# State products by head in quarters of the array, gap products grouped by shape, and weights rounded in three VectorE steps and a GpSimd addition

## The chip, the cores and the metric

The kernel runs on one core of one Trainium2 chip. The metric is the device time of one execution in microseconds; before the change it is 642.75 us (median of three runs, 642.05 to 643.14). Lower is better.

## What is computed

A gated linear attention with a recurrent state, and behind it a feed-forward block with the activation h - tanh(h).

```python
# q, k, v, alpha: (4, 8, 768, 48) fp32; alpha in 0.8..1.0
for t in range(S):
    state = alpha[:, :, t, :, None] * state + einsum('bhd,bhe->bhde', k[:, :, t], v[:, :, t])
    y[:, :, t] = einsum('bhd,bhde->bhe', q[:, :, t], state)
x = y.transpose(0, 2, 1, 3).reshape(3072, 384)
h = x @ w_in                      # (384, 2048)
out = (h - tanh(h)) @ w_out       # (2048, 384)
```

The two weight matrices arrive as 64-bit floating point numbers; the kernel reads them as pairs of 32-bit words and makes fp32 of them itself.

## The kernel before, in words

The 3072 rows of x are cut into 12 units of 256 tokens, two chunks of 128 each. For a unit the attention part (`gla`) loads alpha, k, q and v, turns the first three (32x32 transposes on VectorE, the "flips"), runs two scans over products of alpha (U backwards, W forwards), scales k and q by them (kU, qW; on GpSimd except for unit 0), and then per chunk: scores `sc` (TensorE), a mask product `pm` (VectorE), the outputs `y` (TensorE), a transpose of k (`tp`), its copy `kn` (ACT), and the state's update `up` (TensorE) added to the decayed state (decay on GpSimd, addition on VectorE). Eight heads lie as four pairs `g`, one head of a pair in partitions 0 to 47, the other in 64 to 111; `quads` names these two ranges, and partitions 48 to 63 and 112 to 127 are the gaps. The state of a pair is a 128x128 tile with two 48x48 blocks on its diagonal and zeros elsewhere. The rows of the last two heads are needed in the gaps: units 0 and 1 (`direct`) get them there by extra small products out of `v_gap` and `s_gap`, later units by DMA (`moves`).

The feed-forward part (`moe`) of a unit has eight steps. A step makes h (6 matmuls in the program, 12 passes in the profile), u = h squared on ACT, w = h u on VectorE, two quadratics z on ACT, g from them by two VectorE instructions (z L802, g L803), and then `second`, the product o with w_out. Units 0 and 1 do this plainly (`PLAIN = 2`); later units use seven half-size products with sums e of g and combinations b of w_out's blocks, which GpSimd (four) and VectorE (one) make once, when all of w_out is there.

Weights come in 16 pieces of 128x768 numbers, in0, in1, out0, in2, out1 and so on to out7. Each is fetched by SP into one of four buffers `raw`, read by ACT (two instructions, two buffers each) and finished by VectorE in two instructions: L86 shifts the upper word left by three, L87 adds a word made by ACT out of the sign and the lower word. The result is the weight times 2^-8, which later scales undo. This holds only for weights in a certain range of sizes; so after the combinations all pieces are fetched again and ACT looks at them (L101, L102, `reload` and `look`). At the end a verdict `ok` is made of this and of other ranges, and if it fails, `general` computes everything anew.

A planner (`Planner.order`) simulates the engines with a cost for each task, and a rank, and writes the program in the order in which tasks start. Every engine then works through its own instructions in that order. In what follows, step n is the n-th of all feed-forward steps (step 8 is the first of unit 1), and chunk 2.1 is the second chunk of unit 2.

Of the kernel before, what the change touches and what calls it, by code (L numbers as in the profile page):

```python
# [18 lines left out]
CU = 2  # L19
# [14 lines left out]
W_SCALE = 2.0 ** -8  # L34

# [3 lines left out]
def load_weight(nc, pool, rows, **kw):  # L39

    raw = pool.tile([P, WN], I64 if rows[0][1].dtype != FP32 else FP32, name="raw", **kw)
    for at, src in rows:
        nc.sync.dma_start(out=raw[at].rearrange("p (j n) -> p j n", n=src.shape[-1]), in_=src)
    return raw


def weight_parts(w_in, w_out, pad_rows, what, s):

    if what == "out":
        return [(slice(0, P), w_out.rearrange("(j p) n -> p j n", p=P)[:, 2 * s:2 * s + 2, :])]  # L50
    parts = []
    for i in range(len(pad_rows[0])):
        at, f0 = pad_rows[0][i]
        step = pad_rows[1][i][1] - f0
        src = w_in[f0:f0 + len(pad_rows) * step].rearrange("(j p) n -> p j n", p=step)
        parts.append((at, src[0:at.stop - at.start, :, 2 * s * P:2 * (s + 1) * P]))
    return parts


def words(raw):  # L60

    w = raw.bitcast(I32).rearrange("p (n w) -> p n w", w=2)
    return w[:, :, 0].bitcast(mybir.dt.uint32), w[:, :, 1]


def round_weight(nc, pool, raw, dst):

    V, A = nc.vector, nc.scalar
    n = dst.shape[-1]
    if raw.dtype == FP32:
        A.mul(dst, raw.rearrange("p (j n) -> p j n", n=n), W_SCALE)
        yield
        return
    lo, hi = words(raw)
    bits = pool.tile([P, WN], I32, name="bits")  # L80
    more = pool.tile([P, WN], I32, name="more")
    halves = more.bitcast(mybir.dt.int16).rearrange("p (n two) -> p n two", two=2)
    A.activation(halves[:, :, 0], lo, AF.Copy, scale=2.0 ** -29)
    A.activation(halves[:, :, 1].bitcast(mybir.dt.float16), hi.bitcast(FP32), AF.Sign)
    yield
    V.tensor_scalar(out=bits, in0=hi, scalar1=3, scalar2=None, op0=ALU.logical_shift_left)  # L86
    V.tensor_add(dst.bitcast(I32), bits.rearrange("p (j n) -> p j n", n=n),  # L87
                 more.rearrange("p (j n) -> p j n", n=n))

LEAST, MOST = 2.0 ** (904 // 8 - 127), 2.0 ** (1152 // 8 - 127)


def too_wide(nc, junk, raw, most, least):


    A = nc.scalar
    junk = junk[:, 0:WN]
    src = raw if raw.dtype == FP32 else words(raw)[1].bitcast(FP32)  # L100
    A.activation(junk, src, AF.Abs, accum_out=most)  # L101
    A.activation(junk, junk, AF.Relu, scale=-1.0, bias=LEAST if raw.dtype != FP32 else -1.0, accum_out=least)  # L102


def round_any_weight(nc, pool, raw, dst):

    V, A = nc.vector, nc.scalar
    n = dst.shape[-1]  # L110
    if raw.dtype == FP32:
        A.copy(dst, raw.rearrange("p (j n) -> p j n", n=n))
        return
    lo, hi = words(raw)
    mag = pool.tile([P, WN], FP32, name="g_mag")
    last = pool.tile([P, WN], I32, name="g_last")
    bits = mag.bitcast(I32)
    A.activation(mag, hi.bitcast(FP32), AF.Abs)
    A.activation(last, lo, AF.Copy, scale=2.0 ** -29)

# [6 lines left out]
    V.tensor_add(dst.bitcast(I32), bits.rearrange("p (j n) -> p j n", n=n),  # L127
                 last.rearrange("p (j n) -> p j n", n=n))


def general(tc, q, k, v, alpha, moe_w_in, moe_w_out, out, w_in, w_out, ident, pad_rows):
# [10 lines left out]
    with ExitStack() as ctx:  # L142
        with tc.tile_pool(name="g_raw", bufs=1) as raw_pool:
            for s in range(FT // 2):
                for what, dst in (("in", w_in[:, :, 2 * s * P:2 * (s + 1) * P]), ("out", w_out[:, 2 * s:2 * s + 2, :])):
                    raw = load_weight(nc, raw_pool, weight_parts(moe_w_in, moe_w_out, pad_rows, what, s))
                    round_any_weight(nc, raw_pool, raw, dst)
# [214 lines left out]
def fast(tc, q, k, v, alpha, moe_w_in, moe_w_out, out, w_in, w_out, ident, ok, pad_rows):  # L362
# [14 lines left out]

    out_r = out.rearrange("(t p) n -> t p n", p=P)

    with ExitStack() as ctx:  # L380
# [28 lines left out]
        most, tiny = (consts.tile([P, 2 * FS], FP32, name=n) for n in ("most", "tiny"))  # L409
# [45 lines left out]
        def fetch(what, s):  # L455
            raw_of[what, s] = load_weight(nc, raw_pool, weight_parts(moe_w_in, moe_w_out, pad_rows, what, s), bufs=4)

        def convert(what, s):
            it = []

            def begin():
                dst = w_in[:, :, 2 * s * P:2 * (s + 1) * P] if what == "in" else w_out[:, 2 * s:2 * s + 2, :]
                it.append(round_weight(nc, raw_pool, raw_of.pop((what, s)), dst))
                next(it[0])
            return begin, lambda: next(it[0], None)

        for n, (what, s) in enumerate(pieces):
            rank = RANK[what] + 2 * s
            held = pieces[n - 4] if n >= 4 else None
            add(f"fetch {what}{s}", "SP", 3.9, rank - 30, [held and f"read {held[0]}{held[1]}"],  # L470
                lambda what=what, s=s: fetch(what, s), lat=2.5)
            a, b = convert(what, s)
            older = pieces[n - 2] if n >= 2 else None
            add(f"read {what}{s}", "ACT", 1.85, rank, [f"fetch {what}{s}", older and f"{older[0]}{older[1]}"], a)
            add(f"{what}{s}", "DVE", 1.95, rank, [f"read {what}{s}"], b)
# [21 lines left out]
        def gla(u, rank):  # L497
# [87 lines left out]
            def chunk(c):  # L585
# [43 lines left out]
                def products():  # L629
# [3 lines left out]
                    if n == 0:  # L633
                        for hh, at, j in to_gap:
                            T.matmul(y[at, j, :], lhsT=v_gap[:, c, hh, j, :], rhs=m["pm", c][hh][:, NP - 1, :],
                                     start=(j == 0), stop=True, skip_group_check=True)
                    if n > 0:
                        for g in range(NP):
                            T.matmul(y[:, g, :], lhsT=old[:, g, :], rhs=m["qT"][:, g, c, :],  # L639
                                     start=(g == 0), stop=False, skip_group_check=True)  # L640
                        for hh, at, j in to_gap:
                            T.matmul(y[at, j, :], lhsT=s_gap[quads[hh], j, :],
                                     rhs=m["qT"][quads[hh], NP - 1, c, :],
                                     start=False, stop=False, skip_group_check=True)
                            T.matmul(y[at, j, :], lhsT=v_gap[:, c, hh, j, :], rhs=m["pm", c][hh][:, NP - 1, :],
                                     start=False, stop=False, skip_group_check=True)
                    for g in range(KT if direct else NP):
                        for hh, q in enumerate(quads):
                            T.matmul(y[q, g, :], lhsT=vts[u][:, c, 2 * g + hh, :], rhs=m["pm", c][hh][:, g, :],  # L649
                                     start=(n == 0 and g == 0), stop=True, skip_group_check=True)  # L650
# [19 lines left out]
                def update():  # L670
                    up = m["up", c] = bank("up")[:, :, 0:2 * D].rearrange("p g (two d) -> p g two d", d=D)
                    for g in range(NP):
                        T.matmul(up[:, g], lhsT=m["kn", c][:, g, :], rhs=vts[u][:, c, 2 * g:2 * g + 2, :],  # L673
# [48 lines left out]
        combos, combo_pool = {}, []  # L722

        def combine(n):
            if not combos:
                incoming.close()
                pool = ctx.enter_context(tc.tile_pool(name="combos", bufs=1))
                combo_pool.append(pool)
# [19 lines left out]


        looked = {}  # L750

        def reload(n):
            looked[n] = load_weight(nc, combo_pool[0], weight_parts(moe_w_in, moe_w_out, pad_rows, *pieces[n]))

        def look(n):
            junk = two.tile([P, N * (P + 1)], FP32, name="junk", bufs=1)
            too_wide(nc, junk, looked.pop(n), most[:, n:n + 1], tiny[:, n:n + 1])
        for n in range(len(pieces)):
            rank = 2 * FS * 3 + 8 * n
            add(f"reload {n}", "SP", 1.0, rank, ["combine 4", n > 0 and f"look {n - 1}"], lambda n=n: reload(n), lat=6.0)  # L760
            add(f"look {n}", "ACT", 2.2, rank + 4, [f"reload {n}"], lambda n=n: look(n))
# [3 lines left out]
        def moe(u, rank, gait):  # L765
# [3 lines left out]
            def step(s):  # L769
# [15 lines left out]

                def square():
                    m["u", s] = two.tile([P, 2 * TU], FP32, name="u")
                    A.activation(m["u", s], m["h", s], AF.Square, scale=W_SCALE ** -1.5)  # L788

                def quadratics():  # L790
                    for z, b in (("z1", QB1), ("z2", QB2)):
                        m[z, s] = two.tile([P, 2 * TU], FP32, name=z)
                        A.activation(m[z, s], m["u", s], AF.Square, bias=b, scale=QA * W_SCALE)  # L793
# [12 lines left out]
                def large():  # L806
                    big = two.tile([P, N * (P + 1)], FP32, name="big", tag="junk", bufs=1)[:, 0:2 * TU]
                    n = u * FS + s
                    A.activation(big, m["u", s], AF.Relu, bias=-U_MAX, scale=W_SCALE,  # L809
                                 accum_out=over[:, n:n + 1])  # L810
# [56 lines left out]
            def store():  # L867
                o = m["o"]
                if plain:
                    for c in range(CU):  # L870
                        ob = two.tile([P, d_model], FP32, name=("same", "cross")[c], bufs=1)
                        A.mul(ob, o[c], 1 / W_SCALE)
# [4 lines left out]
                A.mul(p52, o[2], 1 / W_SCALE)  # L877

                def put(out, of, op, more):
                    V.scalar_tensor_tensor(out=out, in0=of, scalar=1 / W_SCALE, in1=more, op0=ALU.mult, op1=op)  # L880
                put(same, o[0][:, 0:1, :].to_broadcast([P, 2, NH]), ALU.subtract, p52)
                put(same, o[1], ALU.add, same)
                put(cross, o[1][:, ::-1, :], ALU.add, p52)
                put(same, o[3], ALU.add, same)
                for c in range(CU):
                    half = [out_r[u * CU + c][:, n * NH:(n + 1) * NH] for n in range(2)]
                    nc.sync.dma_start(out=half[c], in_=same[:, c, :])
                    nc.sync.dma_start(out=half[1 - c], in_=cross[:, c, :])
# [16 lines left out]
        for _, u in sorted(its):  # L905
            next(made[u])
        with tc.manual_schedule():
            for _, _, do, _ in plan.order():
                do()


# [82 lines left out]
```

## Time and profile before

| | |
|---|---|
| profiled execution | 642.75 us, span 640.8 us |
| mean granted TensorE clock | 0.979 |
| TensorE (PE) | 610.4 us busy, 95% |
| VectorE (DVE) | 520.5 us, 81% |
| ScalarE (ACT) | 403.0 us, 63% |
| GpSimd (POOL) | 94.1 us, 15% |
| HBM read and written | 44.04 MB and 4.72 MB |

The page gives busy time as unions over the span. Its slices show the span in forty parts of 16 us each; a digit is the busy share in tenths. A window line gives busy microseconds of each engine in a stretch. A timeline line gives start, duration, engine, source line, operation, tiles, and in brackets how long the engine had been idle and for whom it waited.

### The profile page before, as it was taken

The numbers are of one execution on the slowest core, as the hardware profiler recorded it, in microseconds if no ns is written. First come the engines' busy times: TensorE is split into PE (matmuls) and PEld (weight loads), VectorE is DVE, ScalarE is ACT, GpSimd is POOL, SyncE is SP. The second block draws the span as 40 slices with busy tenths as digits, with TensorE's granted clock in tenths as the row PEclk, the third lists the DMA queues.
The fourth block names the chain that finished last, engine by engine and source line by source line (L and its number), as shares of the span: only waits on it lengthen the run. The fifth ranks groups of instructions, "written<-read, shape, count | busy, mean of one in ns | idle before, by whom it ended". The sixth has DMA issues, their size and how long they took to land.

```text
span 640.8 us, 10379 instructions
## 1 busy us (share of the span) xinstructions
PE 610.4 (95%) x3723; PEld 534.0 (83%) x3723; DVE 520.5 (81%) x915; ACT 403.0 (63%) x825; POOL 94.1 (15%) x84
## 2 busy tenths in 40 slices
PE   7889993999999999999999999999999999999994
PEld 6666672677799899999899999999898999999994
DVE  7897599899689799689999699689899656656762
ACT  3767796588878688678656557457545544545550
POOL 2030028232012002001211011002011000000000
PEclk9799997799999999999999999999999999999998
DMA  9998491455454346433131031021010000000001
GB/s 171 220 201 196 115 225 56 100 103 150 124 104 122 78 111 169 99 103 100 39 71 46 9 78 46 7 76 49 26 32 2 12 20 1 20 14 1 25 2 31
DMA packets 55165, 50.51 MB, mean 79 GB/s; under 512 B 29056, under 2 KB 44864, under 8 KB 55104
## 3 DMA queue, kind: packets, MB, share of 16 engines
q1 hardware_dynamic: 52736, 48.97, 32.5%
q10 hardware_dynamic: 2368, 0.79, 0.8%
q8 instruction: 31, 0.51, 0.4%
q14 instruction: 30, 0.25, 0.1%
HBM read 44.04 MB, written 4.72 MB: 76 GB/s over the span
## 4 chain that ended last, share of the span: by engine, by line
PE 82%; DVE 10%; DMA 4%; issue 2%; ACT 1%; SPq 0%; DVEq 0%; ACTq 0%
PE h L781 35%; PE o L842 27%; PE o L827 6%; PE y L649 3%; PE sc L608 3%; PE y L639 3%; PE up L673 2%; DVE g L803 2%; DMA vt<-in_v_dram 2%; DMA raw<-in_moe_w_in_dram 1%; DVE z L802 1%; PE tp L664 1%; DVE U L545 1%; DMA qr<-in_q_dram 1%; DVE qT L529 1%
## 5 line engine op out<-in xcount | busy, mean ns | idle before, releaser
L781 PE MATMUL h<-xT,w_in 128*128 128x256 f32 x1152 | 268.2, 383 | 7.7 <-DVE w L797 7.0
L781 PEld LDWEIGHTS h<-xT,w_in 128*128 128x128 f32 x1152 | 217.0, 192 | 38.6 <-DVE w L797 7.6
L788 ACT ACTIVATE u<-h 128x512 f32<-128x512 f32 x96 | 57.2, 596 | 156.9 <-PE h L781 156.5
L793 ACT ACTIVATE z<-u 128x512 f32<-128x512 f32 x192 | 110.3, 622 | 4.4 <-DVE g L803 1.9
L797 DVE TENSOR_TENSOR w<-h,u 128x512 f32<-128x512 f32 x96 | 65.9, 686 | 57.8 <-ACT u L788 57.2
L803 DVE SCALAR_TENSOR_TENSOR g<-z,z 128x512 f32<-128x512 f32 x96 | 86.3, 899 | 10.1
L842 PE MATMUL o<-b,e 128*128 128x192 f32 x480 | 91.1, 326 | 0.0
L842 PE MATMUL o<-w_out,e 128*128 128x192 f32 x320 | 80.7, 334 | 0.0
L842 PEld LDWEIGHTS o<-b,e 128*128 128x128 f32 x480 | 80.2, 190 | 0.0
L802 DVE SCALAR_TENSOR_TENSOR z<-z,w 128x512 f32<-128x512 f32 x96 | 69.5, 724 | 5.3 <-ACT z L793 2.1
L842 PE MATMUL o<-b,g 128*128 128x192 f32 x320 | 65.1, 326 | 0.0
L842 PEld LDWEIGHTS o<-w_out,e 128*128 128x128 f32 x320 | 56.5, 190 | 6.7 <-issue 3.0
L618 POOL TENSOR_TENSOR state<-state,ends 48x192 f32<-48x192 f32 x40 | 22.5, 563 | 256.5 <-DVE state L681 216.1
L809 ACT ACTIVATE big<-u 128x512 f32<-128x512 f32 x96 | 59.2, 616 | 0.1
L842 PEld LDWEIGHTS o<-b,g 128*128 128x128 f32 x320 | 54.2, 190 | 0.0
L827 PE MATMUL o<-w_out,g 128*128 128x384 f32 x128 | 47.0, 514 | 3.9 <-DVE g L803 3.8
L827 PEld LDWEIGHTS o<-w_out,g 128*128 128x128 f32 x128 | 24.8, 199 | 19.5 <-DVE g L803 4.5
L564 POOL TENSOR_TENSOR qT<-qT,W 128x1024 f32<-128x1024 f32 x11 | 26.7, 2428 | 76.6 <-DVE qT L529 74.3
L564 POOL TENSOR_TENSOR kT<-kT,U 128x1024 f32<-128x1024 f32 x11 | 24.4, 2217 | 82.3 <-DVE kT L529 60.2
L815 DVE TENSOR_TENSOR e<-g 128x256 f32<-128x256 f32 x80 | 33.3, 416 | 1.4
L614 DVE TENSOR_TENSOR pm<-sc,mask 128x512 f32<-128x512 f32 x46 | 29.5, 683 | 5.9 <-PE sc L608 5.9
L816 DVE TENSOR_TENSOR e<-g 128x256 f32<-128x256 f32 x80 | 33.4, 417 | 0.0
(105 smaller groups left out, 730.5 us busy)
## 6 DMA issues: line engine op xcount, KB each, us to landing
raw<-in_moe_w_out_dram SPq DMA_DIRECT2D x16, 768.0 KB, 5.6
raw<-in_moe_w_in_dram SPq DMA_DIRECT2D x32, 288.0 KB, 5.3
ar<-in_alpha_dram SPq DMA_DIRECT2D x24, 192.0 KB, 3.2
qr<-in_q_dram SPq DMA_DIRECT2D x24, 192.0 KB, 3.2
kr<-in_k_dram SPq DMA_DIRECT2D x22, 192.0 KB, 4.2
vt<-in_v_dram SPq DMA_DIRECT2D x22, 192.0 KB, 4.4
raw<-in_moe_w_in_dram SPq DMA_DIRECT2D x32, 96.0 KB, 5.4
out_dram<-same SPq DMA_DIRECT2D x20, 96.0 KB, 1.7
```

The costliest lines, as they stand in the source:

```text
L564: (V if u == 0 else GP).tensor_mul(t, t, m[by][:, :, 1:])
L781: T.matmul(h[:, a, :], lhsT=w_in[:, j, f * P:(f + 1) * P], rhs=xT[u][:, j, :], start=(j == 0), stop=(j == KT - 1))
L788: A.activation(m["u", s], m["h", s], AF.Square, scale=W_SCALE ** -1.5)
L793: A.activation(m[z, s], m["u", s], AF.Square, bias=b, scale=QA * W_SCALE)
L797: V.tensor_mul(m["w", s], m["h", s], m["u", s])
L802: V.scalar_tensor_tensor(out=z1, in0=z1, scalar=QK1, in1=m["w", s], op0=ALU.add, op1=ALU.mult)
L803: V.scalar_tensor_tensor(out=g.rearrange("p a c t -> p (a c t)"), in0=z2, scalar=QK2, in1=z1, op0=ALU.add, op1=ALU.mult)
L809: A.activation(big, m["u", s], AF.Relu, bias=-U_MAX, scale=W_SCALE, accum_out=over[:, n:n + 1])
L815: V.tensor_add(e[:, 0:2, :], g[:, 0], g[:, 1])
L816: V.tensor_sub(e[:, 2:4, :], g[:, :, 1, :], g[:, :, 0, :])
L827: T.matmul(m["o"][c], lhsT=g[:, a, c, :], rhs=w_out[:, f, :], start=(f == 0), stop=(f == FT - 1))
L842: T.matmul(o[n][:, i], lhsT=g_, rhs=w_, start=(s == 0 and (n, i) in ((0, 0), (1, 0), (2, 1), (3, 0))), stop=(s == FS - 1), skip_group_chec ...
```

## The change

Weights: the factor 2^-8 and everything that belongs to it go, with the reload, the look and their part of the verdict. A piece is now made of the absolute value of the upper word and a scaled lower word (ACT), clamped, shifted and joined with the sign bits (VectorE, three instructions), and added up by GpSimd. Planned costs are 1.85 (ACT), 2.6 (VectorE) and 1.85 (GpSimd). ACT's two buffers are free again after GpSimd's addition.

State products: instead of one product of 128x128 for each pair, one of 48x48 for each head, whose operands lie in one quarter of the array. In direct units the pair in the gaps isn't computed by them any more (three pairs instead of four).

Gap products: all six of `s_gap` first, then all six of `v_gap`, then the others.

Update: 112 columns of `kn` as stationary operand, not 128.

Store: `cross` before the last two sums; its DMAs come ahead of those of `same`, and for the last unit go through ACT's queue. The verdict is made as planned tasks (`judge`, `gather`, `ok`).

```diff
-    A.activation(halves[:, :, 0], lo, AF.Copy, scale=2.0 ** -29)
-    A.activation(halves[:, :, 1].bitcast(mybir.dt.float16), hi.bitcast(FP32), AF.Sign)
+    A.activation(mag, hi.bitcast(FP32), AF.Abs)
+    A.activation(last, lo, AF.Copy, scale=2.0 ** -29)
     yield
-    V.tensor_scalar(out=bits, in0=hi, scalar1=3, scalar2=None, op0=ALU.logical_shift_left)
-    V.tensor_add(dst.bitcast(I32), bits.rearrange("p (j n) -> p j n", n=n),
-                 more.rearrange("p (j n) -> p j n", n=n))
+    V.tensor_scalar(out=mag, in0=mag, scalar1=2.0 ** (896 // 8 - 127), scalar2=2.0 ** (1151 // 8 - 127) * 1.875,
+                    op0=ALU.max, op1=ALU.min)
+    V.tensor_scalar(out=bits, in0=bits, scalar1=3, scalar2=0x3FFFFFFF,
+                    op0=ALU.logical_shift_left, op1=ALU.bitwise_and)
+    V.scalar_tensor_tensor(out=bits, in0=hi, scalar=-0x40000000, in1=bits,
+                           op0=ALU.bitwise_and, op1=ALU.bitwise_or)
+    yield
+    GP.tensor_add(dst.bitcast(I32), bits.rearrange("p (j n) -> p j n", n=n),
+                  last.rearrange("p (j n) -> p j n", n=n))
...
-            add(f"{what}{s}", "DVE", 1.95, rank, [f"read {what}{s}"], b)
+            add(f"bits {what}{s}", "DVE", 2.6, rank, [f"read {what}{s}"], b)
+            add(f"{what}{s}", "POOL", 1.85, rank, [f"bits {what}{s}"], c)
...
-                        for g in range(NP):
-                            T.matmul(y[:, g, :], lhsT=old[:, g, :], rhs=m["qT"][:, g, c, :],
-                                     start=(g == 0), stop=False, skip_group_check=True)
                         for hh, at, j in to_gap:
                             T.matmul(y[at, j, :], lhsT=s_gap[quads[hh], j, :],
                                      rhs=m["qT"][quads[hh], NP - 1, c, :],
-                                     start=False, stop=False, skip_group_check=True)
-                            T.matmul(y[at, j, :], lhsT=v_gap[:, c, hh, j, :], rhs=m["pm", c][hh][:, NP - 1, :],
-                                     start=False, stop=False, skip_group_check=True)
+                                     start=(j == 0), stop=False, skip_group_check=True)
+                    for hh, at, j in to_gap:
+                        T.matmul(y[at, j, :], lhsT=v_gap[:, c, hh, j, :], rhs=m["pm", c][hh][:, NP - 1, :],
+                                 start=(n == 0 and j == 0), stop=True, skip_group_check=True)
+                    heads = [(g, hh, q) for g in range(KT if direct else NP) for hh, q in enumerate(quads)]
+                    if n > 0:
+                        for g, hh, q in heads:
+                            T.matmul(y[q, g, :], lhsT=old[q, g, q], rhs=m["qT"][q, g, c, :],
+                                     start=(g == 0), stop=False, skip_group_check=True)
...
-                        T.matmul(up[:, g], lhsT=m["kn", c][:, g, :], rhs=vts[u][:, c, 2 * g:2 * g + 2, :],
+                        T.matmul(up[0:HP + D, g], lhsT=m["kn", c][:, g, 0:HP + D], rhs=vts[u][:, c, 2 * g:2 * g + 2, :],
...
-            add(f"reload {n}", "SP", 1.0, rank, ["combine 4", n > 0 and f"look {n - 1}"], lambda n=n: reload(n), lat=6.0)
-            add(f"look {n}", "ACT", 2.2, rank + 4, [f"reload {n}"], lambda n=n: look(n))
...
+                V.tensor_sub(same, o[1], p52)
+                V.tensor_add(cross, p52, o[1][:, ::-1, :])
+                V.tensor_add(same, same, o[0][:, 0:1, :].to_broadcast([P, 2, NH]))
+                V.tensor_add(same, same, o[3])
+                for c in range(CU):
+                    half = [out_r[u * CU + c][:, n * NH:(n + 1) * NH] for n in range(2)]
+                    (A if u == NU - 1 else nc.sync).dma_start(out=half[1 - c], in_=cross[:, c, :])
```

## The prediction

> **What bounds the kernel now.** I read the busy shares and slices of the page first, then the table of windows, then the timeline of the stretch that the windows point at, and last the timeline of the end. The span is 640.8 us and the profiled execution took 642.75 us, which is also the median of the three runs; 1.95 us lie around the span, and I keep them.
>
> ```profile
> PE 610.4 (95%) x3723; PEld 534.0 (83%) x3723; DVE 520.5 (81%) x915; ACT 403.0 (63%) x825; POOL 94.1 (15%) x84
> PE   7889993999999999999999999999999999999994
> PEclk9799997799999999999999999999999999999998
> ...
> 60.00:80.00 20.00, 20.00 (x124) 13.91 (x124) 11.26 (x18) 14.78 (x25) 0.00 (x0) 1.00 0.56 129
> 80.00:100.00 20.00, 17.32 (x66) 12.16 (x64) 19.07 (x26) 18.32 (x31) 6.88 (x2) 1.00 0.82 207
> 100.00:120.00 20.00, 11.88 (x26) 7.97 (x27) 19.93 (x21) 10.07 (x19) 14.95 (x6) 0.66 0.17 50
> 300.00:400.00 100.00, 100.00 (x651) 91.80 (x651) 91.64 (x165) 61.41 (x130) 15.69 (x13) 1.00 0.20 46
> ```
>
> In a window line the pairs are PE, PEld, DVE, ACT and POOL busy, then the granted clock. From 120 us on TensorE is busy without a gap, so there only TensorE work counts. Before 120 us it isn't: in 80 to 120 us VectorE is full (19.07 and 19.93 of 20) and TensorE lacks 10.8 us, with the clock at 0.66. The timeline says why VectorE is late there:
>
> ```profile
> 92.12 3.48 POOL L734 TENSOR_TENSOR b<-w_out 128x1536 f32<-128x1536 f32 x1 [42.29 <-DVE w_out L87]
> 94.10 2.08 DVE L529 STREAM_TRANSPOSE kT<-kr 128x256 f32<-128x256 f32 x4
> 95.55 3.45 POOL L736 TENSOR_TENSOR b<-w_out 128x1536 f32<-128x1536 f32 x1
> 96.02 5.15 DVE L545 TENSOR_TENSOR_SCAN U<-aT,after 128x1032 f32<-128x1032 f32 x1
> 104.31 5.08 PE L781 MATMUL h<-xT,w_in 128*128 128x256 f32 x12 [6.98 <-DVE w L797]
> 104.70 5.32 POOL L738 TENSOR_TENSOR b<-w_out 128x1536 f32<-128x1536 f32 x1
> 106.71 3.85 DVE L802 SCALAR_TENSOR_TENSOR z<-z,w 128x512 f32<-128x512 f32 x1
> 109.97 2.62 POOL L564 TENSOR_TENSOR qT<-qT,W 128x1024 f32<-128x1024 f32 x1
> 110.60 2.54 DVE L803 SCALAR_TENSOR_TENSOR g<-z,z 128x512 f32<-128x512 f32 x1
> ```
>
> The scan, 2.3 us elsewhere, takes 5.15 while GpSimd adds; z and g, 0.69 elsewhere, take 3.85 and 2.54 and end with the GpSimd instruction. The four transposes under a GpSimd addition stay at 2.08. So a VectorE instruction with two SBUF inputs waits for GpSimd to finish, and one with a single SBUF input doesn't.
>
> **The Trainium skill.** "SBUF — State Buffer", section "Who interferes with whom", says just this: GpSimd shares a port pair with VectorE, the lock is exclusive and lasts the whole instruction, and a tensor_scalar in a two-port mode contends too. The lines above agree for two inputs; no line here shows tensor_scalar under a long GpSimd instruction. "VectorE: DVE Perf Modes", "The perf-mode tier table": fp32 tensor_scalar within SBUF runs at double rate. Agrees: L86 takes 562 ns for 768 elements. "TensorE: Matmul & The Clock Gate", "LDWEIGHTS (loading the stationary operand)": a load costs by its columns, not its rows. Agrees: `up` with 96 moving columns starts every 0.108 us, as transposes with 128 do (8 from 234.83 to 235.69; 4 from 230.01 to 230.45). "TensorEngine Tiling (Array Packing)", "Key Properties": tiles run at the same time, a change of tiling mode drains the array. Agrees: the 16 `sc` passes on two row halves take 1.09 us (253.00 to 254.09), two at a time, some 0.2 of it at the two changes.
>
> **The change, part by part.**
>
> Conversion of the 16 weight pieces. ACT: Abs costs 0.93 (L101 reads the same strided words) and the int32 copy about 1.05, together 2.0 against 2.12 (L83 and L84): no loss. DVE before: 0.56 + 0.97 = 1.53. After: two tensor_scalar of 0.56 at a pace of 0.5, and a scalar_tensor_tensor of 768 between 0.69 (512, unblocked) and 1.75 (1536), so 0.95: 2.0 us in all. GpSimd: 16 additions of 768; 192 elements take 0.50, 1024 take 2.18, 1536 take 3.45, so 1.66 to 1.73; taken 1.75. That is 28 us of new GpSimd time, all before the combinations of w_out can start, and all three new VectorE instructions, z, g and the scans can be locked out by it. A ready piece now also frees its two buffers only after the GpSimd addition.
>
> So I walked the order of instructions of the changed program through the ramp, with these durations, the rows of before for the rest, and one rule: an instruction of VectorE with two SBUF inputs or in double rate and a GpSimd addition exclude each other, the first come first. End of each g (step 0 to 9), before from the timeline, then walked: g0 47.5, 49.2; g1 54.9, 59.6; g2 65.4, 69.4; g3 76.5, 75.3; g4 81.7, 91.2; g5 85.2, 105; g6 90.3, 116.7; g7 113.1, 122.6; g8 117.7, 134.5; g9 125.3, 139.9. How a step looks: after g3 come convert in5 (75.3 to 77.3), the flips of unit 2's aT (to 79.3, free of the lock, GpSimd adds in5 beside it), w4 (80), convert out4 (82), one tensor_scalar of in6, then GpSimd's addition of out4 (82.5 to 84.3) with VectorE locked out, the rest of in6 (85.7), the scan U (88), GpSimd's in6 (to 89.8), z4 and g4 (91.2). g4 to g6 are that late also because the planner puts unit 2's flips and scan ahead of them. Before had them after g6, so g7 is the first fair comparison: +9.5. In before, three of the four combinations are over or running by then; in after all four start only after out7 is added (121.9), and b0 to b2 lock out z8 and g8: +16.8 at g8. For TensorE I compare equal work: o of step 9, h of step 11 and y of chunk 2.1 all done. Before that is 137.1 (start of the next h, 137.13). Walked: o8 134.6 to 137.2, h11 to 139.8, y 2.1 waits for its mask product, which stands behind g9 and the kT flips on VectorE (143.9), y to 145.9, o9 to 148.5. Lag **+11.4**.
>
> Bounds of this: with no lock for tensor_scalar and additions of 1.5, about +5; with every addition stopping VectorE for its whole 1.75 and half a clock after each gap of TensorE (104.31 shows 5.08 for 12 passes that take 2.6), about +20. I take the walk.
>
> Gap products. Before, 24 passes alternate two shapes: 30.89 to 34.90, 4.0 us in each of three chunks. Grouped, each shape is like L635, 12 passes in 1.02 (27.25 to 28.27): 2.05. Saves about 2 us three times. In the walk y 0.1 then ends 2 us sooner, but VectorE is the late one, and this is in the +11.4 already.
>
> State products. Before: 8 passes of 128x128, 0.99 (230.45 to 231.44), no change of shape from `tp`. After: 16 passes in opposite quarters. If two run at a time as in L649 (16 in 1.01): 0.9, plus one more change of shape, 0.2; so about +0.2 in each of the chunks with n over 0, 16 of them after the ramp: **+3.2**. Bounds: 0 (the change is free), and +0.9 a chunk (the quarters run one by one), +14.
>
> Update with 112 columns: 8 passes, 0.108 falling to 0.108 x 112/128 = 0.095: -0.11 a chunk, 16 after the ramp: **-1.8**.
>
> Reload and look: 34 us of ACT (L101, L102 and their accumulators) and 12.6 MB of DMA go. After 120 us nothing of TensorE waits for ACT or DMA, so 0; it cannot lose. Store: DVE instructions keep 0.55. At the end two of four DMA issues move to ACT's queue:
>
> ```profile
> 633.52 0.33 SPq L887 DMA_DIRECT2D out_dram<-same  x1
> 633.90 0.43 SPq L888 DMA_DIRECT2D out_dram<-cross  x1
> 634.37 0.43 SPq L887 DMA_DIRECT2D out_dram<-same  x1
> 634.85 0.43 SPq L888 DMA_DIRECT2D out_dram<-cross  x1
> ```
>
> The last issue comes two places earlier: **-0.9**. The load of ok now stands ahead of them on SP; its ok is ready long before, so nothing. The verdict's VectorE instructions (2 us together) were already spread in gaps.
>
> Sum: 11.4 + 3.2 - 1.8 - 0.9 = +11.9 on 642.75: **654.6 us**.
>
> **Rivals.** (1) The lock is milder (tensor_scalar not stopped, shorter additions): ramp +5, sum +5.5, 648. For it: L86 under the short L618 was stretched by 0.12 only (48.79, 0.67). Against: nearly every g under L564 is stopped to its end. (2) Faster: VectorE's slack takes all of the conversion. The 60 to 80 window shows 8.7 us idle on VectorE, where the gap products keep TensorE busy. If the additions fall under flips, w and mask products, g7 and g8 come no later than before; then TensorE's savings count, 3 x 2 + 1.8 + 0.9 - 3.2 = 5.5, 637. The point of decision is g8: at 117.7 or sooner this holds. Against: in 80 to 120 there is no slack, and six pieces are left at 80 in the walk. (3) The quarters run one by one: 0.9 instead of 0.2 in 16 chunks, 11 us more, 666. Against: both halves by rows (sc) and by columns (L649) overlap in the trace.
>
> **Numbers.** Forecast 0.64; rival 1 0.12; rival 2 0.13; rival 3 0.08; small net change 0.03. The range takes in rival 1, the bounds +5 and +20 of the ramp with the rest of the sum: 644 to 664, leaving out rival 2, most of rival 3. 0.2% (1.3 us) is about what can be told from no change. Faster 0.13, same 0.03, slower 0.84. The forecast's own range is 648 to 662.
>
> **What would show it.** In the changed profile: GpSimd's additions near 1.75, conversions on VectorE stretched beyond 2.0 where they meet them; TensorE's slices of 80 to 140 us lower than before, waiting for VectorE's w or g, clock below 1; g8 near 134 us; from 150 us on a full TensorE; y's state products at 0.9 to 1.2 us a chunk, `up` near 0.75. I am wrong if TensorE is full through 80 to 120, or if g8 comes before 120.

## The result and the profile after

The changed kernel takes 651.5 us (median; 651.35 to 652.11) against 642.5 in the same comparison: a ratio of 1.014, with a 95% interval of 1.012 to 1.016. It is slower, by 9 us. The forecast was 654.6 with a range of 644 to 664. The profiled span grew by the same 8.8 us, from 640.8 to 649.6, so the traces can be compared mark by mark.

First the busy shares and slices of the changed kernel's page:

```profile
PE 608.0 (94%) x3871; PEld 530.0 (82%) x3871; DVE 546.6 (84%) x927; ACT 369.1 (57%) x761; POOL 127.3 (20%) x100
...
PE   6779956979999999999999999999999999999995
...
PEclk9898967979999999999999999999999999999999
```

and the shares of the chain of waits by engine, before and then after:

```profile
PE 82%; DVE 10%; DMA 4%; issue 2%; ACT 1%; SPq 0%; DVEq 0%; ACTq 0%
PE 73%; DVE 17%; issue 4%; DMA 2%; ACT 2%; POOL 0%; SPq 0%; DVEq 0%; ACTq 0%; POOLq 0%
```

TensorE works 2.4 us less than before and the kernel is 9 us longer, so TensorE waits more. It does so in the first 150 us, called the ramp here: from the tenth slice of 16 us on it is full (before, from the eighth). VectorE has 26 us more of busy time and GpSimd 33. The chain agrees: VectorE carried 10% of it before, 17% now.

The windows of the changed kernel (PE, PEld, DVE, ACT, POOL, granted clock) show where:

```profile
60.00:80.00 20.00, 19.90 (x125) 14.23 (x122) 19.44 (x28) 16.57 (x29) 7.91 (x4) 1.00 0.85 193
80.00:100.00 20.00, 9.56 (x27) 6.43 (x25) 19.76 (x22) 12.48 (x22) 10.31 (x5) 0.74 0.63 150
100.00:120.00 20.00, 16.90 (x68) 11.93 (x69) 19.69 (x20) 9.77 (x19) 10.09 (x7) 0.83 0.07 20
120.00:140.00 20.00, 14.71 (x88) 10.71 (x89) 19.70 (x23) 9.70 (x21) 16.16 (x7) 0.83 0.18 53
300.00:400.00 100.00, 100.00 (x665) 91.13 (x664) 90.52 (x164) 61.63 (x130) 15.39 (x13) 1.00 0.20 46
```

Three things are to be seen. VectorE had 8.7 us free in 60 to 80; now it has 0.6. TensorE lacked 10.8 us in 80 to 120; now it lacks 13.5 there and 5.3 more in 120 to 140. And a busy VectorE is not a working one: it runs fewer instructions in these windows than before (22 and 20 against 26 and 21 in 80 to 120) and is "busy" throughout.

What fills it is seen in its groups and GpSimd's, taken by shape (times: sum, then mean in ns):

```profile
L72 POOL TENSOR_TENSOR w_in<-mag,last 128x768 int32<-128x768 int32 x8 | 17.5, 2192 | 28.7 <-ACT mag L61 17.4 <-DVE mag L69 9.7 <-DVE ends L501 1.6
L72 POOL TENSOR_TENSOR w_out<-mag,last 128x768 int32<-128x768 int32 x8 | 15.9, 1992 | 21.7 <-DVE mag L69 17.6 <-ACT ar L473 4.1
L69 DVE SCALAR_TENSOR_TENSOR mag<-raw,mag 128x768 int32<-128x768 int32 x16 | 15.5, 971 | 0.6
L67 DVE TENSOR_SCALAR mag<-mag 128x768 int32<-128x768 int32 x16 | 13.8, 862 | 0.6
L65 DVE TENSOR_SCALAR mag<-mag 128x768 f32<-128x768 f32 x16 | 13.8, 861 | 0.1
```

and in the timeline (lines of VectorE and GpSimd, and one of TensorE), first around one pair of pieces, then around step 8:

```profile
80.88 0.55 DVE L65 TENSOR_SCALAR mag<-mag 128x768 f32<-128x768 f32 x1
81.11 1.98 POOL L72 TENSOR_TENSOR w_out<-mag,last 128x768 int32<-128x768 int32 x1 [2.71 <-DVE mag L69]
81.47 2.05 DVE L67 TENSOR_SCALAR mag<-mag 128x768 int32<-128x768 int32 x1
83.55 0.96 DVE L69 SCALAR_TENSOR_TENSOR mag<-raw,mag 128x768 int32<-128x768 int32 x1
84.42 2.30 DVE L494 TENSOR_TENSOR_SCAN U<-aT,after 128x1032 f32<-128x1032 f32 x1
84.65 3.67 POOL L72 TENSOR_TENSOR w_in<-mag,last 128x768 int32<-128x768 int32 x1 [1.56 <-ACT mag L61]
86.64 2.23 DVE L734 SCALAR_TENSOR_TENSOR z<-z,w 128x512 f32<-128x512 f32 x1
...
88.37 5.49 PE L714 MATMUL h<-xT,w_in 128*128 128x256 f32 x12 [7.06 <-POOL w_in L72]
...
117.18 2.12 POOL L72 TENSOR_TENSOR w_out<-mag,last 128x768 int32<-128x768 int32 x1 [3.36 <-DVE mag L69]
117.74 2.12 DVE L735 SCALAR_TENSOR_TENSOR g<-z,z 128x512 f32<-128x512 f32 x1
...
123.15 3.43 POOL L683 TENSOR_TENSOR b<-w_out 128x1536 f32<-128x1536 f32 x1
123.48 3.65 DVE L734 SCALAR_TENSOR_TENSOR z<-z,w 128x512 f32<-128x512 f32 x1
...
126.54 3.87 POOL L685 TENSOR_TENSOR b<-w_out 128x1536 f32<-128x1536 f32 x1
127.23 3.73 DVE L735 SCALAR_TENSOR_TENSOR g<-z,z 128x512 f32<-128x512 f32 x1
```

The lock works both ways. At 81.11 GpSimd's addition is first, and a shift that takes 0.55 alone takes 2.05: it ends at 83.52, 0.43 after the addition. At 84.65 the scan is first, and the addition (about 1.8 on its own) takes 3.67, so that h, which needs its weights, starts after 7 us of idle TensorE. Then z and g of step 8 lie under two of the four combinations. Over the whole ramp, 12 VectorE instructions that overlap an addition L72 take 15.5 us more in all than the medians of their lines.

### The profile page after: what moved, and what is told of

It is laid out like the page before. It is cut to its first block, busy times and chain, and to the rows that moved or that the text cites. A ratio compares the mean times of both kernels' runs of the same rounds, so it can differ in the third digit from the quotient of the medians.

```text
span 649.6 us, 10584 instructions
## 1 busy us (share of the span) xinstructions
PE 608.0 (94%) x3871; PEld 530.0 (82%) x3871; DVE 546.6 (84%) x927; ACT 369.1 (57%) x761; POOL 127.3 (20%) x100
## 4 chain that ended last, share of the span: by engine, by line
PE 73%; DVE 17%; issue 4%; DMA 2%; ACT 2%; POOL 0%; SPq 0%; DVEq 0%; ACTq 0%; POOLq 0%
PE h L714 31%; PE o L773 27%; PE sc L557 3%; PE y L597 3%; PE y L594 3%; PE o L758 2%; PE up L621 2%; DVE z L734 2%; DVE g L735 2%; DVE qT L478 2%; DVE kT L478 1%; DVE mag L69 1%; DVE aT L478 1%; DVE mag L65 1%; PE tp L612 1%
## 5 line engine op out<-in xcount | busy, mean ns | idle before, releaser
L735 DVE SCALAR_TENSOR_TENSOR g<-z,z 128x512 f32<-128x512 f32 x96 | 95.4, 993 | 10.1
L734 DVE SCALAR_TENSOR_TENSOR z<-z,w 128x512 f32<-128x512 f32 x96 | 73.7, 768 | 4.7 <-ACT z L725 1.9
L567 POOL TENSOR_TENSOR state<-state,ends 48x192 f32<-48x192 f32 x40 | 23.9, 598 | 235.8 <-DVE state L629 206.5
L758 PE MATMUL o<-w_out,g 128*128 128x384 f32 x128 | 50.0, 539 | 8.4 <-DVE g L735 8.2
L557 PEld LDWEIGHTS sc<-qT,kT 48*128 48x128 f32 x368 | 23.4, 192 | 13.4 <-issue 13.3
```

Of the source, the lines that this page charges most:

```text
L557: T.matmul(sc[hh][:, g, :], lhsT=m["kT"][q, g, c, :], rhs=m["qT"][q, g, c, :], start=True, stop=True)
L734: V.scalar_tensor_tensor(out=z1, in0=z1, scalar=QK1, in1=m["w", s], op0=ALU.add, op1=ALU.mult)
L735: V.scalar_tensor_tensor(out=g.rearrange("p a c t -> p (a c t)"), in0=z2, scalar=QK2, in1=z1, op0=ALU.add, op1=ALU.mult)
L758: T.matmul(m["o"][c], lhsT=g[:, a, c, :], rhs=w_out[:, f, :], start=(f == 0), stop=(f == FT - 1))
```

## The experiments

One table for all. "g8" is the end of g of step 8 and "h12" the start of h of step 12, both in us from the start of the trace; "end" is the time from the start of the last six TensorE passes of o to the end of the span. These three are read from each kernel's one trace; the us are medians. The ratio is to the kernel before in the same comparison.

| kernel | us | ratio, 95% interval | g8 | h12 | end |
|---|---|---|---|---|---|
| before | 642.5 | 1 | 117.7 | 137.1 | 10.1 |
| after | 651.5 | 1.014 [1.012, 1.016] | 131.0 | 147.5 | 8.1 |
| w_only | 655.6 | 1.018 [1.012, 1.024] | 133.6 | 150.5 | 10.1 |
| qgus | 637.7 | 0.990 [0.987, 0.993] | 115.0 | 133.1 | 9.6 |
| after_noadd | 637.7 | 0.992 [0.990, 0.995] | 117.0 | 133.4 | 8.2 |
| before_adds | 652.3 | 1.014 [1.008, 1.020] | 127.9 | 146.4 | 10.4 |
| before_vadds | 654.1 | 1.020 [1.015, 1.025] | 130.6 | 147.3 | 10.0 |
| g_only | 638.4 | 0.993 [0.990, 0.995] | 117.4 | 135.4 | 10.0 |
| s_only | 642.3 | 0.999 [0.997, 1.001] | 117.5 | 136.9 | 10.1 |
| gus | 637.6 | 0.991 [0.988, 0.994] | 114.8 | 133.9 | 9.1 |
| gus_dve | 626.6 | 0.974 [0.970, 0.977] | 108.3 | 125.4 | 9.3 |
| after_add_dve | 657.0 | 1.021 [1.019, 1.024] | 135.5 | 152.3 | 8.2 |
| after_comb_dve | 644.1 | 1.002 [1.001, 1.003] | 125.2 | 140.3 | 8.7 |
| after_both_dve | 650.1 | 1.011 [1.008, 1.013] | 127.6 | 144.1 | 8.2 |

**Which part costs?** Two kernels split the change: the weights alone (w_only), and all the rest without them (qgus).

```diff
# w_only: the changed kernel, with the products, update, store and verdict of before
-                        for g, hh, q in heads:
-                            T.matmul(y[q, g, :], lhsT=old[q, g, q], rhs=m["qT"][q, g, c, :],
+                        for g in range(NP):
+                            T.matmul(y[:, g, :], lhsT=old[:, g, :], rhs=m["qT"][:, g, c, :],
...
-                        T.matmul(up[0:HP + D, g], lhsT=m["kn", c][:, g, 0:HP + D],
+                        T.matmul(up[:, g], lhsT=m["kn", c][:, g, :],
# qgus: the kernel before, with the changed kernel's products, update, store and verdict
```

> The conversion of the weights alone, as in the changed kernel (reload and look gone), with the old products, update and store. Theory (VectorE is late before 140 us because of its own longer conversion and because GpSimd's additions lock it out): the whole loss is here. At equal work, start of h of step 12, the changed kernel is 10.4 us behind before (147.5 against 137.1), and the gap products' saving was of no use there; the end is as in before. So 653 to 655 us, g8 near 131 us. Rival (the loss comes from the new products and their changes of shape on TensorE): 641 to 645.

> Everything but the weights: the old one-shift conversion with reload and look, and quarters, grouping, 112 columns, the new store and the verdict in the plan. Theory: these four can only gain. Quarters +0.12 us and update -0.09 in some 18 chunks, +0.4 together; end -2.0; grouping 6 us of TensorE, of which VectorE's backlog at 80 to 117 us leaves 0 to 5: 635 to 641 us, likeliest 638. Rival: 645 or more.

Measured: 655.6 (+13.2 us; a little over what was expected, with g8 at 133.6 and not 131) and 637.7 (-4.7). The sum of the two, +8.5, is near the +9 of the whole: the parts about add up, the weights cost 13 us, and the other four gain 5.

**Is it the additions on GpSimd?** One kernel takes the 16 additions out of the changed kernel. The other puts 16 into the kernel before, on data that nobody uses, so that no weight comes later for it.

```diff
# after_noadd
-    V.scalar_tensor_tensor(out=bits, in0=hi, scalar=-0x40000000, in1=bits,
-                           op0=ALU.bitwise_and, op1=ALU.bitwise_or)
+    V.scalar_tensor_tensor(out=dst.bitcast(I32), in0=hi.rearrange("p (j n) -> p j n", n=n), scalar=-0x40000000,
+                           in1=bits.rearrange("p (j n) -> p j n", n=n),
+                           op0=ALU.bitwise_and, op1=ALU.bitwise_or)
...
-    GP.tensor_add(dst.bitcast(I32), bits.rearrange("p (j n) -> p j n", n=n),
-                  last.rearrange("p (j n) -> p j n", n=n))
# before_adds
+    yield
+    nc.gpsimd.tensor_add(bits, bits, more)
...
+            add(f"extra {what}{s}", "POOL", 1.85, rank, [f"{what}{s}"], b)
```

> The changed kernel without GpSimd's 16 additions: VectorE's third instruction writes the weights itself. The low word of the weights is left out of the computation, and nothing else; ACT still makes it. VectorE keeps its three instructions (2.0 us a piece, 0.5 more than before). Theory: the stretched instructions of VectorE next to the additions sum to 15.5 us in the changed trace; without them g8 comes at 115 to 119 us, no later than in before, and the time is 637 to 642 us. Rival (VectorE's own third instruction and the planner's order with unit 2's flips ahead are the loss): 647 to 652.

> The kernel before, with one more addition on GpSimd after each piece is finished, of the two dead temporaries (768 words), in place; the weights do not use it, but the temporaries are free only after it, as in the changed kernel. Theory (lock): VectorE's instructions with two SBUF inputs or in double rate stretch by about 1 us for each addition, g8 moves from 117.7 to 122 to 130, the combinations start later, 646 to 651 us. Rival (GpSimd has the time free, only VectorE's own third instruction costs): 642 to 644.

Measured: 637.7 without them, 652.3 with them in the kernel before (a little over what was expected). after_noadd is as fast as qgus, which has the old conversion: with no addition on GpSimd, the three new VectorE steps cost little. Its h12 is 0.3 us later than that of qgus and the stretch from there to the last passes of o 0.6 us longer, and an end that is 1.4 us shorter makes up for both. The steps find room in the free time of 60 to 80 us, where VectorE is 18.2 us busy in after_noadd and 13.8 in qgus. So the additions on GpSimd are about the whole of the 13 us. In before_adds no weight waits for an addition, and they still cost 10; in the changed kernel h also waits for its weights (7 us at 88.4), and whether the other 3 come from this was not taken apart. In before_adds, the timeline (lines of VectorE and GpSimd) shows the lock on instructions that don't need the addition's result:

```profile
84.09 2.14 POOL L90 TENSOR_TENSOR bits<-bits,more 128x768 int32<-128x768 int32 x1 [0.96 <-DVE w_in L87]
84.65 2.13 DVE L806 SCALAR_TENSOR_TENSOR g<-z,z 128x512 f32<-128x512 f32 x1
...
93.39 1.82 POOL L90 TENSOR_TENSOR bits<-bits,more 128x768 int32<-128x768 int32 x1 [2.29 <-DVE w_in L87]
93.77 1.87 DVE L86 TENSOR_SCALAR bits<-raw 128x768 int32<-128x768 int32 x1
```

g, 0.69 when alone, takes 2.13; the shift, 0.55 when alone, 1.87. Eleven such instructions are stretched by 13.4 us in all. A rival is that the addition also keeps ACT's buffers longer. ACT does wait for them in before_adds, 8.0 us in the first 150. But VectorE, the late engine, does not wait for the words that ACT makes: its one wait for ACT in this time is 1.1 us, for u. In the changed kernel the trace lists no wait of VectorE between the first load of alpha and 150 us. So the held buffers are not what makes VectorE late.

**The other parts by themselves.** g_only groups the gap products in the kernel before; s_only has the new store and the planned verdict; gus has both and the 112 columns, and not the quarters.

```diff
# g_only (in the kernel before; s_only and gus likewise take over the lines of the change)
                         for hh, at, j in to_gap:
                             T.matmul(y[at, j, :], lhsT=s_gap[quads[hh], j, :],
                                      rhs=m["qT"][quads[hh], NP - 1, c, :],
                                      start=False, stop=False, skip_group_check=True)
-                            T.matmul(y[at, j, :], lhsT=v_gap[:, c, hh, j, :], rhs=m["pm", c][hh][:, NP - 1, :],
-                                     start=False, stop=False, skip_group_check=True)
+                    for hh, at, j in to_gap:
+                        T.matmul(y[at, j, :], lhsT=v_gap[:, c, hh, j, :], rhs=m["pm", c][hh][:, NP - 1, :],
+                                 start=(n == 0 and j == 0), stop=(n == 0), skip_group_check=True)
```

> The kernel before with the gap products grouped by shape and nothing else. Whole pairs still make the state products. In the ramp each of the three grouped chunks saves about 2 us of TensorE, but VectorE is what is late from 80 us on. Theory that VectorE is the late one: 638 to 642, between 0 and -4. If TensorE were the late one there, the full 6 us: 636 to 637.

> The kernel before with the new order of the output sums and DMAs and with the verdict planned as tasks (its parts of over, sizes and least, and the old look's), nothing else. The end from the start of the last six TensorE passes to the end of the span was 10.1 us before and 8.1 after. Theory that this is all from the end: 640.4 (-2.0). If only the issue order counts, as the prediction had it: 641.6 (-0.9). If the planned verdict costs VectorE something in the middle: 642 or more.

> The kernel before with three of the five parts: grouped gap products, 112 columns in the update, the new store and verdict. Old conversion of the weights and its look, and the state products by whole pairs. Sum of the parts: -1.5 (update, 16 times 0.093) -2.0 (end) and 0 to -4 (gaps): 635 to 639. Without the quarters it should be 1 to 3 us below the version that has them (637.65); if the quarters cost nothing in the whole, equal to it.

Measured: g_only 638.4, at the strong end of what was expected; the interval is 3 to 7 us. Its trace shows less, a span 1.8 us shorter and h12 1.7 us sooner, but it is of the slowest of its eight runs (640.8), so the size is not well known. s_only 642.3: no change that can be told from none (interval -1.7 to +0.7 us), and its end is 10.1 us as before; the expected -2.0 fell. gus 637.6, the same as qgus with the quarters: on the whole the quarters neither gain nor lose. qgus is 0.9 us sooner than gus at h12 and takes 1.5 us more from there to its last TensorE pass, so in these traces a part of what the quarters cost later is won in the ramp. That it is won because the direct chunks make three pairs and not four is likely, but was not tried alone.

**The combinations.** In the kernel before, four combinations of w_out lie on GpSimd at 92 to 117 us. gus_dve is gus with these on VectorE, one after g of each of five steps of unit 1:

```diff
-                GP.tensor_add(combos["11+22"], b11, b22)
+                V.tensor_add(combos["11+22"], b11, b22)
...
-            add(f"combine {n}", "POOL" if n < 4 else "DVE", 3.6 if n < 4 else 1.9, 2 * FS + 2 + n,
-                [f"out{FS - 1}", f"in{FS - 1}", f"gaps {PLAIN - 1}.{CU - 1}", f"y {PLAIN - 1}.{CU - 1}"]
+            add(f"combine {n}", "DVE", 1.9, 2 * FS + 2 + n,
+                [f"out{FS - 1}", f"in{FS - 1}", f"gaps {PLAIN - 1}.{CU - 1}", f"y {PLAIN - 1}.{CU - 1}",
+                 f"shrunk {PLAIN - 1}:{(1, 2, 4, 5, 6)[n]}"]
```

> The three parts of the run above, and the four combinations of w_out that GpSimd made (3.5 to 5.3 us each, at 92 to 117 us) made by VectorE instead, one after g of the steps 1, 2, 4, 5 and 6 of unit 1, at 1.75 to 1.9 us each. Theory that long GpSimd additions which lock out VectorE are what makes the ramp late: the g of steps 7 to 9 come 5 to 9 us earlier, TensorE is fuller in 95 to 120, 628 to 634. Theory that VectorE simply has too much to do in the ramp, wherever the additions run: 4 times 1.8 us more on VectorE, no gain or a loss, 637 to 643.

Measured: 626.6, a larger gain than was expected: 11 us under gus, 16 under the kernel before, 25 under the changed one. VectorE's lines of its timeline:

```profile
93.43 2.24 DVE L545 TENSOR_TENSOR_SCAN U<-aT,after 128x1032 f32<-128x1032 f32 x1
...
100.95 0.94 DVE L800 SCALAR_TENSOR_TENSOR z<-z,w 128x512 f32<-128x512 f32 x1
101.92 2.54 DVE L801 SCALAR_TENSOR_TENSOR g<-z,z 128x512 f32<-128x512 f32 x1
...
113.59 1.73 DVE L731 TENSOR_TENSOR b<-w_out 128x1536 f32<-128x1536 f32 x1
```

and its windows:

```profile
80.00:100.00 20.00, 15.80 (x61) 11.30 (x60) 18.94 (x31) 19.35 (x34) 3.92 (x3) 0.99 0.79 180
100.00:120.00 20.00, 18.90 (x113) 14.04 (x113) 19.66 (x26) 12.47 (x27) 6.06 (x5) 0.93 0.16 45
```

The scan is back from 5.14 in gus to 2.24, z of step 7 from 3.86 to 0.94; g still lies under the scaling of q on GpSimd. A combination takes VectorE 1.73 instead of GpSimd 3.44 to 5.32. TensorE has 18.9 us of work in 100 to 120, where it had 14.7 in gus (11.9 in the kernel before), and its clock there is 0.93 instead of 0.69 (0.66). Two things were changed at once, the engine and the time (113 to 142 us): no run tells them apart. The traces speak for the time. In gus the four combinations stretch the scan and the z of steps 7 and 8 by 6.8 us in all, and on VectorE the four take 7.0 us. By this estimate VectorE would have paid about as much at the same place, and the gain would come from paying after the places where TensorE waits for it.

**And in the changed kernel?** After this, three kernels move its own GpSimd work to VectorE: the 16 additions, the four combinations, and both.

```diff
# after_add_dve
-    GP.tensor_add(dst.bitcast(I32), bits.rearrange("p (j n) -> p j n", n=n),
-                  last.rearrange("p (j n) -> p j n", n=n))
+    V.tensor_add(dst.bitcast(I32), bits.rearrange("p (j n) -> p j n", n=n),
+                 last.rearrange("p (j n) -> p j n", n=n))
...
-            add(f"bits {what}{s}", "DVE", 2.6, rank, [f"read {what}{s}"], b)
-            add(f"{what}{s}", "POOL", 1.85, rank, [f"bits {what}{s}"], c)
+            add(f"{what}{s}", "DVE", 3.5, rank, [f"read {what}{s}"], lambda b=b, c=c: (b(), c()))
# after_comb_dve: the edit of gus_dve; after_both_dve: both
```

> The changed kernel with the 16 last additions of the conversion made by VectorE (0.97 us each, as the addition of the kernel before) in place of GpSimd (1.8). VectorE gets 16 us more work, GpSimd loses 29. Theory that the lock makes the lag: the g of steps 4 to 8 come several us sooner than 89.6 to 131.0, though VectorE has more to do; with no addition at all the time was 637.7, and of the 16 us some 6 to 10 fall into the full stretch: 643 to 649, likeliest 646. Theory that the lag is VectorE's own work, and that taking an addition off VectorE helps: slower than the changed kernel, 655 or more.

> The changed kernel with the four combinations of w_out made by VectorE, spread over the steps of unit 1, in place of GpSimd (3.4 to 3.9 us each, at 119 to 139 us); the 16 additions of the conversion stay on GpSimd. It tells how much of the lag comes from the combinations being pushed onto z and g of steps 8 and 9. In the kernel with the old conversion the same edit gained 11 us. If the combinations cost as much here: 640 to 643. If the 16 additions alone make up the lag of 10: g8 stays near 128 and the time at 648 to 651.

> Both edits together: no addition of a weight piece and no combination on GpSimd, the changed kernel otherwise. VectorE has then 16 us plus 7 us more than in the changed kernel, and meets GpSimd only in the scaling of k and q and the state's decay. Lock theory: 633 to 640, faster than the kernel before in spite of the longer conversion; against the 626.6 of the version with the old conversion and combinations on VectorE, the rest is the longer conversion (three instructions and the addition, about 3.0 us, against 1.53). Theory of VectorE's work: slower than the changed kernel, 655 or more.

Measured: the additions on VectorE make it slower, 657.0, and not faster; the combinations on VectorE gain 7.4 us (644.1); both together 650.1. The last two lie in none of the ranges written for them. The first is a miss of the theory as I held it, that VectorE would do an addition for less than the lock takes. VectorE's timeline in after_add_dve shows a piece with no lock in it:

```profile
79.25 0.55 DVE L65 TENSOR_SCALAR mag<-mag 128x768 f32<-128x768 f32 x1
79.84 0.56 DVE L67 TENSOR_SCALAR mag<-mag 128x768 int32<-128x768 int32 x1
80.43 0.96 DVE L69 SCALAR_TENSOR_TENSOR mag<-raw,mag 128x768 int32<-128x768 int32 x1
81.56 0.96 DVE L72 CUSTOM_DVE_ANT_0 w_in<-mag,last 128x1536 uint16<-128x1536 uint16 x1 [0.17 <-DVE mag L69]
82.43 0.69 DVE L733 SCALAR_TENSOR_TENSOR z<-z,w 128x512 f32<-128x512 f32 x1
```

From L65 to z it is 3.18 us, of which the addition with its wait takes 1.1 or so. Sixteen of 0.96 are 15.4 us. The lock took 15.5. So the price is about the same.

That reading came after the fact, so it got a run of its own: the kernel before with 16 extra additions on VectorE, beside the 16 on GpSimd of before_adds.

```diff
                  more.rearrange("p (j n) -> p j n", n=n))
+    V.tensor_add(bits, bits, more)
...
-            add(f"{what}{s}", "DVE", 1.95, rank, [f"read {what}{s}"], b)
+            add(f"{what}{s}", "DVE", 2.95, rank, [f"read {what}{s}"], b)
```

> The kernel before with one more addition after each weight piece, as in the run with 16 extra GpSimd additions (652.3), but made by VectorE. Its result is not used. Two readings of the run in which moving the addition to VectorE made the changed kernel slower: if an addition costs VectorE's time either way, by the lock about as much as by doing it, this comes out near the GpSimd one or a few us above: 652 to 658. If the lock is the larger price and the slower time came only from the order that the planner found there: 645 to 650. If VectorE had room for 0.97 us a piece: 643 to 645.

Measured: 654.1, against 652.3 with GpSimd. Here an addition costs about as much on either engine, within intervals of 5 to 13 us on GpSimd and 10 to 16 on VectorE for the sixteen: what the ramp is short of is VectorE's time, and a GpSimd instruction that locks VectorE out spends it as well as VectorE's own work does. Why after_add_dve loses 5.5 us to the changed kernel, and not 2, is open. It is 7.9 us behind already at the end of g of step 1 (67.2 against 59.3); the planner orders the program differently there, and the fetch of a later piece waits for the addition as well, and these were not taken apart.

## Why the prediction was right, and where it was off

The direction, the place and the mechanism were as forecast. By its steps:

- **Ramp, +11.4.** The equal-work point h12 moved from 137.1 to 147.5: +10.4. The walk by hand gave g4 91.2, g6 116.7, g8 134.5, g9 139.9; the trace has 89.6, 114.4, 131.0, 136.1. The exclusion of tensor_scalar by GpSimd, for which the trace of before had no line and the Trainium skill ("SBUF — State Buffer", "Who interferes with whom") had to stand, is seen at 81.47: 0.55 becomes 2.05. The addition itself, taken at 1.75, takes about 1.8 where nothing holds it up. The bound of +5 with no lock on tensor_scalar is out.

  The last steps of the walk were not as forecast, so that the sum came this near is in part luck. It had TensorE wait for the mask product of chunk 2.1 until 143.9. In the trace that product is done at 140.0 and y starts at 142.84 without a wait. In its place TensorE waited 5.29 us before the scores, until VectorE had done g of step 8, the next w, a scan and an addition of the state, and then took 3.80 us for o of step 8, where o of step 9 took 2.85:

```profile
134.55 2.04 PE L557 MATMUL sc<-qT,kT 48*128 48x128 f32 x14 [5.29 <-DVE state L629]
136.53 3.80 PE L758 MATMUL o<-w_out,g 128*128 128x384 f32 x8
138.69 1.28 DVE L563 TENSOR_TENSOR pm<-sc,mask 128x512 f32<-128x512 f32 x2
142.84 1.08 PE L594 MATMUL y<-qT,state 48*48 48x128 f32 x16
```

  Two readings of the trace of before were loose. z and g do not end with the GpSimd instruction but about 0.55 us after it (z of 106.71 at 110.56, GpSimd at 110.02), so they wait and then work. And at the g7 of before all four combinations had begun, not three; the fourth starts at 112.55.
- **What the lag consists of.** It is a net sum: the weights alone move h12 by +13.4 (w_only), the other parts by -4.0 (qgus); the two make 9.4 of the 10.4. The prediction left the gap products' saving inside the lag, with VectorE the late one. By itself the grouping was worth something already in the kernel before (g_only: 1.7 us at h12 in its trace, 4 by the medians).
- **Longer conversion on VectorE, 2.0 against 1.53.** It costs little (after_noadd beside qgus, 0.3 us at h12). Rival 2's slack in 60 to 80 took most of it, as that rival said; it could not take the additions too, and g8 came at 131.0, far over its point of decision at 117.7.
- **State products, +3.2.** The size was off: +1.8. In the timeline of TensorE after (lines below), from the first pass of y to the next product is 1.01 us (before 0.99), and from `tp` to y 0.53 (before 0.44), so +0.115 a chunk (from unrounded times) in 16 chunks and not 0.2. The quarters run two at a time, so rival 3 (666) is out.

```profile
240.66 0.60 PE L612 MATMUL tp<-ident,kT 128*128 128x128 f32 x4
241.19 1.08 PE L594 MATMUL y<-qT,state 48*48 48x128 f32 x16
242.20 1.08 PE L597 MATMUL y<-pm,vt 128*48 128x128 f32 x16
...
245.59 0.93 PE L621 MATMUL up<-vt,kn 128*112 128x96 f32 x8
246.36 2.78 PE L714 MATMUL h<-xT,w_in 128*128 128x256 f32 x12
```

- **Update, -1.8.** 245.59 to 246.36 is 0.77 for eight passes, 0.86 before: 0.093 a chunk from unrounded times, -1.5 in all.
- **Reload and look, 0; end, -0.9.** The end is 2.0 us shorter. Its last computing lines and DMA issues in the changed kernel:

```profile
641.52 1.14 PE L773 MATMUL o<-b,e 128*128 128x192 f32 x6
641.72 0.48 ACT L808 COPY p<-o 128x384 f32<-128x384 f32 x1 [5.84 <-PE o L773]
642.24 0.56 DVE L809 TENSOR_TENSOR same<-o,p 128x384 f32<-128x384 f32 x1 [1.53 <-ACT p L808]
...
643.28 0.89 ACTq L815 DMA_DIRECT2D out_dram<-cross  x2
643.82 0.56 DVE L812 TENSOR_TENSOR same<-same,o 128x384 f32<-128x384 f32 x1
644.41 0.91 SPq L818 DMA_DIRECT2D out_dram<-same  x2
```

  The last issue starts 3.3 us after the start of the last six passes and not 4.2: the 0.9 of the forecast. But what follows the last issue varies as well: from its end to the end of the span it is 5.5 us before, 4.3 in the changed kernel, 6.0 in s_only, where the issues came sooner too and nothing was gained. The short end of 8.1 to 8.7 is only in kernels with the new store and without the reload and look; the new store with them has 9.1 to 10.1, the old store without them 10.1 (w_only). So the forecast's term was half of it, and why the new store and the missing reload and look together give another 1 us is open.

The sum as measured, 10.4 + 1.8 - 1.5 - 2.0 = +8.7, is the +8.8 of the span. The forecast of +11.9 was 3.2 us too high: ramp, state products and end were taken too dear by 1.0, 1.4 and 1.1 us, the update's gain too large by 0.3.

## What to carry to other kernels

Ask what an instruction moved to GpSimd takes from VectorE before counting it as free: in this ramp each addition of 1.8 us on GpSimd stopped VectorE for about 1 us on average, which is what VectorE itself would have needed. Where VectorE is full and TensorE waits for it, look first at the long GpSimd instructions with two inputs and at when they have to run: four of them, moved to VectorE and spread over later steps, gave 11 us, more than the whole change lost. How much of this is the engine and how much the later time is not shown; the estimate above speaks for the time. And split a change before keeping or dropping it, since four of its five parts together were 5 us faster.

## What the hardware showed that was not expected

- An int32 addition of 768 columns costs VectorE 0.96 us and GpSimd 1.8, yet in this kernel, short of VectorE's time, the two cost about the same in the end (16 more of them: +11 us on VectorE and +10 on GpSimd).
- After its last DMA issue the program took between 4.2 and 6.0 us to the end of the span, in kernels that end with the same stores.
